# Bucketed attention and a rational feed-forward layer: sums, hash bits and a scaling put at other places in a hand-written order of work

## The chip, the cores and the metric

One core of one Trainium2 chip. The metric is the device time of one execution in microseconds (us). The kernel before took 917.11 us in the median of 3 runs (916.74 to 922.86).

## The reference

```python
# q, k, v: (4, 8, 768, 64); proj: (64, 6)
q_bucket = sum over 6 bits of 2**i * (q @ proj > 0)        # k_bucket likewise
mask = q_bucket[..., :, None] == k_bucket[..., None, :]
scores = where(mask, q @ k.T / 8, -1e9)
attn = exp(scores - max(scores)); attn /= sum(attn) + 1e-9
x = (attn @ v) laid out as (3072, 512)
# feed-forward: w_in (512, 2048), w_out (2048, 512), a (4), b (2)
h = x @ w_in
P = a0 + a1*h + a2*h*h + a3*h*h*h
Q = 1 + |b0|*|h| + |b1|*h*h
out = (P / (Q + 1e-6)) @ w_out
```

## The kernel before, in words

The 32 heads are worked on as 16 pairs, p = 0 to 15. A pair has 12 steps. A step (`scores`, lines 357 to 382) multiplies 128 keys with 384 queries for both heads, two matmuls a head (tile pss), and ScalarE takes the exponential of each head's 128x384 into one of nine buffers E. GpSimd adds the exponentials of six steps up into acc, one acc for each half of the queries (three acc buffers). `values` (384 to 391) multiplies a step's exponentials with v on a 64-column half of the TensorE array for each head (psv). In a middle pair (`group=6` in MID) the values of six steps are done in one go: steps 0 to 5 behind step 5, which are called the first values here, and steps 6 to 11 behind step 11, the second values. `values_out` (393 to 398) is ScalarE's scaling of the result into xo: a copy of one column (col) and an activation of 128x384. `values_store` sends xo to DRAM. `sums` (403 to 412) adds acc over its 128 rows with 32-column matmuls (psu, 8 matmul records) and copies the result to sr on ScalarE; `sums_store` sends it out in two DMAs of 3 KB; `recips` (421 to 432) reads it back for every fourth pair.

While pair p is worked on, later pairs are prepared. `load` (120 to 124) brings q and k, transposed, into qkf (two buffers). `high` (217 to 221) rounds them on ScalarE, `low` (227 to 230) takes the rest on VectorE, and `high_move`, `second_low`, `second_high` move halves between partitions by DMA. `bits` (244 to 257) multiplies q and k of two pairs with the projection (psb, 32 columns, 16 matmul records, in every other pair) and compares on VectorE; `penalties` and `maskrows` turn the bits into extra rows of q and k. `maxstep` (271 to 281) finds the row maxima: two matmuls (psm) and a VectorE reduction (m) for each of 12 steps. `shift_turn` transposes them (pst), `shift_rows` (294 to 300) puts them into a row of q by DMA.

The feed-forward weights are float64 and are converted in the same stretch (`weights`, 437 to 481, a generator of up to eight pieces: load, ScalarE pieces, VectorE pieces on the PSUM tile psx, a rounding with a PSUM copy psz, a subtraction, for w_out a store). After the attention comes the feed-forward layer: `Gemm1` (psh), the rational terms, `gemm2` (pso).

PSUM: the tag "s" has three banks, which pss, psu, psx, psz and the transposes share in turn; psm and psb share two double banks; psv has one bank. So the second head's scores of a step wait until the first head's exponential of the step before is done, three banks back.

The order of everything in the attention is written by hand. `at(p, s, f)` (487 to 488) puts a call at position 12 p + s, where s may be a fraction and may lie beyond the pair; all calls are sorted by position (608 to 610), and each engine and the DMA queue keep that order. The positions stand in the tables MID, FIRST (pairs 0 and 1 and what prepares pairs 0 to 2) and LAST (pairs 14 and 15). At the positions that matter here:

```python
at(p, s, scores, p, s)                                   # step s of pair p
at(p, s + MID["values"][s // n], values, p, i)           # 5.66 and 11.05
at(p, s + MID["values_out"][s // n], values_out, p, s // NT)   # 5.69 and 11.06
at(p, MID["sums"], sums, p)                              # 14.65: pair p+1, behind its third step
at(p - 2, MID["bits"], bits, p)                          # 2.81 of pair p-2
at(p - 2, MID["high"][1], high, p, 1)                    # k's rounding, 1.19 of pair p-2
at(p - 2, MID["low"][t + t * p % 2], low, p, t, ...)     # 1.06 and 3.3 or 3.35
```

Of the kernel before, what the change touches and what calls it, by code (L numbers as in the profile page):

```python
# [13 lines left out]
ALU = mybir.AluOpType  # L14
# [11 lines left out]
NPAIR = B * NHP  # L26
# [13 lines left out]
BANKED = (2, 29)  # L40

MID = dict(
    group=6, values=[0.66, 0.05], values_out=[0.69, 0.06],
    maxima=[6.54, 7.17, 8.32, 9.1, 10.1, 11.02, 12.25, 13.03, 14.15, 15.17, 16.01, 17.43], sums=14.65, sums_store=17.37,
    high=[-0.975, 1.19], low=[1.06, 3.3, 3.35], bits=2.81, penalties=4.02, high_move=1.9, maskrows=4.03, second_low=-2.2,
    second_high=2.69, load_v=10.99, shift_turn=5.67, shift_rows=8.82, load=4.04, recips=[20.0, 35.02, 35.3],
    weights=[[1.44, 5.1, 5.5, 5.65, 5.66, 11.02, 11.023], [8.05, 11.021, 11.022, 11.024, 11.0245, 17.63, 17.665, 19.32, 21.22]],
    weights_last=[0.5, 0.8, 1.0, 1.2],
)

FIRST = dict(
    maxima1=[-0.072, -0.05, 5.52, 5.97, 6.42, 6.87, 7.32, 7.77, 8.22, 8.67, 9.12, 9.57], maxima2=9.5, rate2=0.82, high=[3.25, 3.53],
    low=[6.0, 7.3], bits=7.4, penalties=7.45, high_move=4.53, maskrows=8.2, second_low=-24.19, second_high=4.35, load_v=4.78, group=2,
    values=[-1.07, 2.65, 2.32, 2.35, 0.35, 0.61], values_out=3.02, high1=[-3.0, -3.2], low1=[-2.8, -2.95],
    high_move1=-2.7, load2=-2.6, load3=3.8, load4=9.0, penalties1=-24.26, maskrows1=-24.2,
    weights=[[-27.25, 6.64, 6.7, 7.35, 12.19, 17.55, 18.33], [8.03, 9.04, 9.24, 9.25, 14.81, 15.27, 15.99, 17.91, 46.81]],
    warm0=9, warm1=1, warm=3, warms=[3, 3, 3, 0, 1, 0], maxima00=[-4.3, -2.3, -4.2, -0.9, -1.2, -0.8], shift00=[-1.0, -0.2],
    shift0=[-0.08, -0.075], ahead=3, scores=[[-0.85, -0.4, -0.1], [0.1, 0.3, 0.4]], pen01=[-2.9, -0.35],
    second_high0=[-3.42, -3.4, -3.3, -3.25], load_v0=-3.3, bits1=-0.3, comp1=[-0.28, -0.27],
    maxima0=[-24.05, -23.8, -23.5, -0.9, -0.7, -0.1], turn1=[8.46, 13.26], rows1=[9.59, 14.35], turn2=8.61, third=6.9,  # L60
    third_weights=[1.44, 5.1, 5.5, 5.65, 5.66, 11.02, 11.023], steps={3: -1.0, 4: -0.8, 5: -0.6, 6: 5.4, 7: 6.5},
)

LAST = dict(
    group=6, values=[0.28, 0.44], values_out=0.46, vout14=[3.5, 3.03],
    hi14=17.05, weights15=[5.1, 5.11],
    tokens=[[-15.0, -11.5, -8.6, -4.9], [-7.43, -4.5, -2.83, -1.09], [1.1, 4.2, 5.45, 6.3]], terms=1.0, ffn=[13.61, 16.09, 16.14],
    sums=16.96, wide=8, share=6, third=0, sums14=14.69, weights14=1.44, sumst14=22.46,
# [32 lines left out]
def move(nc, out, in_, queue=None):  # L101

    (queue or nc.sync).dma_start(out.bitcast(F32), in_.bitcast(F32))
# [3 lines left out]
def bucket_attention_then_rational_ffn(ctx, tc, qT, kT, v, proj, w_in, w_out, coef, consts, out):  # L107
# [56 lines left out]
    def operands_to_terms():  # L164
# [3 lines left out]

    tail.tile([P, 32], F32, tag="below", name="below")
    last = attention(tc, nc, raw, ps_b, tail, tokens, early, operands_to_terms, ffn, load, QF, KF, v, w_in, w_out, wo_d, ident, cst,  # L170
                     ones, prj, wi_hi, wi_lo, x_d, s_d, r_d, coefficients)
    ffn.rest(ctx, last)
# [3 lines left out]
def attention(ctx, tc, nc, raw, ps_b, tail, tokens, early, operands_to_terms, ffn, load, QF, KF, v, w_in, w_out, wo_d, ident, cst, ones, prj,  # L176
# [257 lines left out]
    def bank(name):  # L434
        return ps_b.tile([P, 512], F32, tag="s", bufs=3, name=name)

    def weights(i):

        if i % 2 == 0:
            f, cc = divmod(i // 2, 4)
            sl = slice(f * 512, f * 512 + 512)
            src, hi, lo = w_in[cc * P : cc * P + P, sl], wi_hi[:, cc, sl], wi_lo[:, cc, sl]
        else:
            src, hi, lo = w_out[i // 2 * P : i // 2 * P + P, :], None, None
        r = sm.tile([P, 2 * 512], F32, tag="wr", name=f"wr{i}", bufs=2)
        t = sm.tile([P, 512], F32, tag="ws", name=f"ws{i}", bufs=2)
        if src.dtype == F32:
            nc.sync.dma_start(t, src)  # L450
            yield
        else:
            nc.sync.dma_start(r.bitcast(I32), src.bitcast(I32))
            yield
            hw, lw = r[:, 1:1024:2], r[:, 0:1024:2]
            nc.scalar.activation(t, hw, AF.Copy, scale=2.0 ** -112)
            yield
            nc.scalar.activation(lw.bitcast(I32), lw.bitcast(U32), AF.Copy, scale=2.0 ** -29)
            x, y = hw.bitcast(I32), t.bitcast(I32)
            if BANKED[0] <= i < BANKED[1]:  # L460
                x = y = bank(f"psx{i}").bitcast(I32)
            nc.vector.tensor_scalar(out=x, in0=hw.bitcast(I32), scalar1=-(1 << 31), scalar2=None, op0=ALU.bitwise_and)
            yield
            nc.vector.scalar_tensor_tensor(out=y, in0=t.bitcast(I32), scalar=3, in1=x, op0=ALU.logical_shift_left,
                                           op1=ALU.bitwise_or)
            yield
            nc.vector.tensor_tensor(out=t.bitcast(I32), in0=y, in1=lw.bitcast(I32), op=ALU.add)
            yield
        if hi is None:
            hi, lo = r[:, 0:512].bitcast(F32R), r[:, 512:1024].bitcast(F32R)  # L470
        nc.scalar.copy(hi, t)
        z = hi.bitcast(F32)
        if BANKED[0] <= i < BANKED[1]:
            z = bank(f"psz{i}")
            nc.scalar.copy(z, hi.bitcast(F32))
        yield
        nc.vector.tensor_tensor(out=lo, in0=t, in1=z, op=ALU.subtract)
        yield
        if i % 2 == 1:
            move(nc, wo_d[i // 2], r.rearrange("p (t c) -> p t c", t=2))  # L480
            yield
# [5 lines left out]
    def at(p, s, f, *args):  # L487
        plan.setdefault(12 * p + s, []).append((f, args))

    def spread(p, steps, gen):  # L490
        for s in steps:
            at(p, s, lambda g: next(g, None), gen)

    for p in range(NPAIR):
        mid = 0 < p < NPAIR - 1
        n = MID["group"] if mid else (FIRST if p == 0 else LAST)["group"]
        for s in range(12):
            if p > 0 or s >= FIRST["ahead"]:
                at(p, FIRST["steps"].get(s, s) if p == 0 else s, scores, p, s)

            if p > 1:
                at(p - 2, FIRST["maxima2"] + FIRST["rate2"] * s if p == 2 else FIRST["third"] if p == 3 and s == 0 else MID["maxima"][s], maxstep, p, s)
            if s % n == n - 1:
                for i in range(s - n + 1, s + 1):
                    at(p, s + (MID["values"][s // n] if mid else (FIRST if p == 0 else LAST)["values"][s // n]), values, p, i)
            if s % NT == NT - 1:
                at(p, s + (LAST["vout14"][s // NT] if p == NPAIR - 2 else MID["values_out"][s // n] if mid else (FIRST if p == 0 else LAST)["values_out"]), values_out, p, s // NT)
        for hf in range(2):
            at(p, 6 * hf + 9, values_store, p, hf)
        if p < NPAIR - 1:  # L510
            at(p, MID["sums"] if p < NPAIR - 2 else LAST["sums14"], sums, p)
            at(p, MID["sums_store"] if p < NPAIR - 2 else LAST["sumst14"], sums_store, p)
        if p > 1:
            for t in range(2):
                at(p - 2, (MID if p > 2 else FIRST)["high"][t], high, p, t)
                at(p - 2, MID["low"][t + t * p % 2] if p > 2 else FIRST["low"][t], low, p, t, nc.vector if p > 2 else nc.gpsimd)
            if p % 2 == 0:
                at(p - 2, (MID if p > 2 else FIRST)["bits"], bits, p)
                at(p - 2, (MID if p > 2 else FIRST)["penalties"], penalties, p)
            at(p - 2, (MID if p > 2 else FIRST)["high_move"], high_move, p)  # L520
            at(p - 2, (MID if p > 2 else FIRST)["maskrows"], maskrows, p)
        if p > 0:
            at(p - 1, (MID if p > 1 else FIRST)["second_low"], second_low, p)
            at(p - 1, (MID if p > 1 else FIRST)["second_high"], second_high, p)
            at(p - 1, (MID if p > 1 else FIRST)["load_v"], load_v, p)
        if p > 1:
            at(p - 1, MID["shift_turn"] if p > 2 else FIRST["turn2"], shift_turn, p)
            at(p - 1, MID["shift_rows"], shift_rows, p)
        if p > 3:
            at(p - 4, MID["load"] if p > 4 else FIRST["load4"], load, p)  # L530
        if p % NHP == NHP - 1 and p + 1 < NPAIR:
            spread(p, MID["recips"], recips(p // NHP))
# [325 lines left out]
```

## Time and profile before

| | |
|---|---|
| median of 3 runs | 917.11 us (916.74 to 922.86) |
| profiled execution, its own time | 916.53 us |
| span of its instructions | 914.7 us |
| granted TensorE clock | 1.000 over the span |
| busy: TensorE, VectorE, ScalarE, GpSimd | 907.4, 818.0, 669.4, 438.7 us |

The span is from the first to the last instruction of the program; 1.8 us of the time lie around it. Durations of matmuls are modelled, and they overlap, so the distance from one start to the next tells what a matmul costs, not the duration of a row. A row of a timeline merges neighbouring instructions of the same kind. All times are us from the start of the span.

### The profile page before, as it was taken

The numbers are of one execution on the slowest core, as the hardware profiler recorded it, in microseconds if no ns is written. First come the engines' busy times: TensorE is split into PE (matmuls) and PEld (weight loads), VectorE is DVE, ScalarE is ACT, GpSimd is POOL, SyncE is SP. The second block draws the span as 40 slices with busy tenths as digits, with TensorE's granted clock in tenths as the row PEclk, the third lists the DMA queues.
The fourth block names the chain that finished last, engine by engine and source line by source line (L and its number), as shares of the span: only waits on it lengthen the run. The fifth ranks groups of instructions, "written<-read, shape, count | busy, mean of one in ns | idle before, by whom it ended". The sixth has DMA issues, their size and how long they took to land.

```text
span 914.7 us, 13736 instructions
## 1 busy us (share of the span) xinstructions
PE 907.4 (99%) x4543; PEld 694.8 (76%) x4543; DVE 818.0 (89%) x1043; ACT 669.4 (73%) x1254; POOL 438.7 (48%) x408
## 2 busy tenths in 40 slices
PE   9999999999999999999999999999999999999998
PEld 5567777676767676678888888888888888888886
DVE  7888888888888887989999999999999989998997
ACT  7467878887878787886677766776677677677664
POOL 7688888888888887012322232222322222222221
PEclk9999999999999999999999999999999999999999
DMA  7787878787878778456204000400040012001001
GB/s 215 202 217 226 235 213 248 218 244 212 242 224 241 195 215 242 137 202 198 95 1 138 1 1 1 138 1 1 0 138 1 1 56 83 1 1 47 1 0 47
DMA packets 51243, 111.57 MB, mean 122 GB/s; under 512 B 9346, under 2 KB 20214, under 8 KB 51172
## 3 DMA queue, kind: packets, MB, share of 16 engines
q1 hardware_dynamic: 50740, 110.47, 40.9%
q8 instruction: 36, 0.59, 0.3%
q14 instruction: 35, 0.29, 0.1%
q10 hardware_dynamic: 432, 0.23, 0.1%
HBM read 56.82 MB, written 21.17 MB: 85 GB/s over the span
## 4 chain that ended last, share of the span: by engine, by line
PE 97%; DVE 1%; DMA 1%; issue 0%; SPq 0%; ACT 0%; DVEq 0%
PE psh L96 29%; PE pso L96 29%; PE pss L96 15%; PE psv L96 14%; PE psm L96 7%; PE psu L96 1%; PE psb L96 1%; DVE m L96 1%; DMA qkf<-kT 0%; DMA k<-lo 0%; SPq L96 0%; PE pst_None L96 0%; PE pst L96 0%; PE psw L96 0%; DVE ws L96 0%
## 5 line engine op out<-in xcount | busy, mean ns | idle before, releaser
L96 POOL TENSOR_TENSOR gl<-c,gh 128x512 fp32r<-128x512 f32 x95 | 136.9, 1441 | 408.2 <-ACT gh L96 399.0
L96 PE MATMUL pso<-wo,gh 128*128 128x512 f32 x768 | 235.9, 389 | 0.0
L96 POOL TENSOR_TENSOR acc<-acc,E 128x384 f32<-128x384 f32 x232 | 219.6, 982 | 5.9 <-ACT E L96 5.8
L96 DVE TENSOR_REDUCE m<-psm 128x1 f32<-128x768 f32 x192 | 181.1, 954 | 46.1 <-PE psm L96 37.7
L96 ACT ACTIVATE E<-pss 128x384 f32<-128x384 f32 x384 | 167.5, 492 | 43.0 <-PE pss L96 28.4
L96 PE MATMUL pss<-q,k 128*128 128x384 f32 (+2 forms) x768 | 172.9, 348 | 0.1
L96 PEld LDWEIGHTS pso<-wo,gh 128*128 128x128 f32 x768 | 144.2, 188 | 29.9
L96 ACT ACTIVATE h<-psh 128x512 f32<-128x512 f32 x96 | 57.4, 598 | 133.7 <-PE psh L96 133.7
L96 PEld LDWEIGHTS pss<-q,k 128*128 128x128 f32 (+2 forms) x768 | 133.9, 189 | 24.4 <-issue 6.8
L96 PE MATMUL psh<-xh,wi_hi 128*128 128x512 f32 x384 | 149.6, 390 | 0.0
L96 PE MATMUL psh<-xh,wi_lo 128*128 128x512 f32 x384 | 149.4, 389 | 0.0
L96 PE MATMUL psh<-xl,wi_hi 128*128 128x512 f32 x384 | 149.4, 389 | 0.0
L96 PE MATMUL pso<-wo,gl 128*128 128x512 f32 x384 | 148.9, 389 | 0.0
L96 DVE SCALAR_TENSOR_TENSOR c<-c,ab,r 128x512 f32<-128x512 f32 x96 | 140.8, 1467 | 0.0
L96 PE MATMUL psv<-E,v 128*64 128x385 f32 x768 | 131.9, 492 | 0.0
L96 PE MATMUL psm<-k,q 76*128 76x384 f32 (+1 forms) x384 | 100.7, 344 | 2.0 <-DVE m L96 0.6
L96 PEld LDWEIGHTS psv<-E,v 128*64 128x64 f32 x768 | 52.0, 137 | 65.1 <-issue 63.3
L96 POOL TENSOR_TENSOR acc<-E,E 128x384 f32<-128x384 f32 x58 | 68.8, 1205 | 48.7 <-ACT E L96 48.7
L96 DVE SCALAR_TENSOR_TENSOR w<-h,absb,w 128x512 f32<-128x512 f32 x96 | 73.9, 770 | 16.2 <-ACT w L96 15.8
L96 PEld LDWEIGHTS psh<-xh,wi_hi 128*128 128x128 f32 x384 | 72.0, 187 | 16.1 <-ACT r L96 0.6
L96 PEld LDWEIGHTS psh<-xh,wi_lo 128*128 128x128 f32 x384 | 72.1, 188 | 15.0
L96 PEld LDWEIGHTS pso<-wo,gl 128*128 128x128 f32 x384 | 72.0, 188 | 15.0
(87 smaller groups left out, 1184.4 us busy)
## 6 DMA issues: line engine op xcount, KB each, us to landing
q<-q SPq DMA_DIRECT2D x45, 192.0 KB
k<-k SPq DMA_DIRECT2D x45, 192.0 KB
wr<-w_in SPq DMA_DIRECT2D x16, 512.0 KB
wr<-w_out SPq DMA_DIRECT2D x16, 512.0 KB
wo_d<-wr SPq DMA_DIRECT2D x16, 512.0 KB
wo<-wo_d SPq DMA_DIRECT2D x16, 512.0 KB
qkf<-qT SPq DMA_DIRECT2D x16, 384.0 KB
qkf<-kT SPq DMA_DIRECT2D x16, 384.0 KB
```

What stands on the lines that cost most here:

```text
L96: return self.tc.keep_in_program_order(issue(*args, **kwargs))
```

## The change

The positions of several calls are moved. `sums` of pair p goes from behind the third step of pair p+1 to directly ahead of that pair's first values (14.65 to 17.62), its store from 17.37 to 18.9, and the reading back from 20.0 to 21.5. `bits` goes from 2.81 of a pair to -0.945, directly behind the second values of the pair before it. The scaling of the second values goes from directly behind them (0.06) to behind the third step of the next pair (3.25), its store from 15 to 16.6. Three pieces of the even weights' conversion go from 5.5, 5.65 and 5.66 to 5.657, 5.658 and 5.659, behind the sums. In the first pairs: the pieces of weight 0 and its subtraction, the latter from VectorE to GpSimd; one DMA step of pair 1 (`rows1`, 9.59 to 8.6); the first `low` of pair 3 (1.06 to 1.9).

```diff
--- before.py
+++ after.py
@@ -40,11 +40,11 @@
 BANKED = (2, 29)
 
 MID = dict(
-    group=6, values=[0.66, 0.05], values_out=[0.69, 0.06],
-    maxima=[6.54, 7.17, 8.32, 9.1, 10.1, 11.02, 12.25, 13.03, 14.15, 15.17, 16.01, 17.43], sums=14.65, sums_store=17.37,
-    high=[-0.975, 1.19], low=[1.06, 3.3, 3.35], bits=2.81, penalties=4.02, high_move=1.9, maskrows=4.03, second_low=-2.2,
-    second_high=2.69, load_v=10.99, shift_turn=5.67, shift_rows=8.82, load=4.04, recips=[20.0, 35.02, 35.3],
-    weights=[[1.44, 5.1, 5.5, 5.65, 5.66, 11.02, 11.023], [8.05, 11.021, 11.022, 11.024, 11.0245, 17.63, 17.665, 19.32, 21.22]],
+    group=6, values=[0.66, 0.05], values_out=[0.69, 3.25],
+    maxima=[6.54, 7.17, 8.32, 9.1, 10.1, 11.02, 12.25, 13.03, 14.15, 15.17, 16.01, 17.43], sums=17.62, sums_store=18.9,
+    high=[-0.975, 1.19], low=[1.06, 3.3, 3.35], bits=-0.945, penalties=4.02, high_move=1.9, maskrows=4.03, second_low=-2.2,
+    second_high=2.69, load_v=10.99, shift_turn=5.67, shift_rows=8.82, load=4.04, recips=[21.5, 35.02, 35.3],
+    weights=[[1.44, 5.1, 5.657, 5.658, 5.659, 11.02, 11.023], [8.05, 11.021, 11.022, 11.024, 11.0245, 17.63, 17.665, 19.32, 21.22]],
     weights_last=[0.5, 0.8, 1.0, 1.2],
 )
 
@@ -53,13 +53,15 @@
     low=[6.0, 7.3], bits=7.4, penalties=7.45, high_move=4.53, maskrows=8.2, second_low=-24.19, second_high=4.35, load_v=4.78, group=2,
     values=[-1.07, 2.65, 2.32, 2.35, 0.35, 0.61], values_out=3.02, high1=[-3.0, -3.2], low1=[-2.8, -2.95],
     high_move1=-2.7, load2=-2.6, load3=3.8, load4=9.0, penalties1=-24.26, maskrows1=-24.2,
-    weights=[[-27.25, 6.64, 6.7, 7.35, 12.19, 17.55, 18.33], [8.03, 9.04, 9.24, 9.25, 14.81, 15.27, 15.99, 17.91, 46.81]],
+    weights=[[-27.25, 5.45, 5.98, 5.99, 11.9, 17.55, 18.3], [8.03, 9.04, 9.24, 9.25, 14.81, 15.27, 15.99, 17.91, 46.81]],
     warm0=9, warm1=1, warm=3, warms=[3, 3, 3, 0, 1, 0], maxima00=[-4.3, -2.3, -4.2, -0.9, -1.2, -0.8], shift00=[-1.0, -0.2],
     shift0=[-0.08, -0.075], ahead=3, scores=[[-0.85, -0.4, -0.1], [0.1, 0.3, 0.4]], pen01=[-2.9, -0.35],
     second_high0=[-3.42, -3.4, -3.3, -3.25], load_v0=-3.3, bits1=-0.3, comp1=[-0.28, -0.27],
-    maxima0=[-24.05, -23.8, -23.5, -0.9, -0.7, -0.1], turn1=[8.46, 13.26], rows1=[9.59, 14.35], turn2=8.61, third=6.9,
-    third_weights=[1.44, 5.1, 5.5, 5.65, 5.66, 11.02, 11.023], steps={3: -1.0, 4: -0.8, 5: -0.6, 6: 5.4, 7: 6.5},
+    maxima0=[-24.05, -23.8, -23.5, -0.9, -0.7, -0.1], turn1=[8.46, 13.26], rows1=[8.6, 14.35], turn2=8.61, third=6.9,
+    third_weights=[1.44, 5.1, 5.657, 5.658, 5.659, 11.02, 11.023], steps={3: -1.0, 4: -0.8, 5: -0.6, 6: 5.4, 7: 6.5},
 )
+
+FIRST3 = dict(low=[1.9, 3.3, 3.35])
 
 LAST = dict(
     group=6, values=[0.28, 0.44], values_out=0.46, vout14=[3.5, 3.03],
@@ -474,7 +476,7 @@
             z = bank(f"psz{i}")
             nc.scalar.copy(z, hi.bitcast(F32))
         yield
-        nc.vector.tensor_tensor(out=lo, in0=t, in1=z, op=ALU.subtract)
+        (nc.vector if i else nc.gpsimd).tensor_tensor(out=lo, in0=t, in1=z, op=ALU.subtract)
         yield
         if i % 2 == 1:
             move(nc, wo_d[i // 2], r.rearrange("p (t c) -> p t c", t=2))
@@ -506,14 +508,14 @@
             if s % NT == NT - 1:
                 at(p, s + (LAST["vout14"][s // NT] if p == NPAIR - 2 else MID["values_out"][s // n] if mid else (FIRST if p == 0 else LAST)["values_out"]), values_out, p, s // NT)
         for hf in range(2):
-            at(p, 6 * hf + 9, values_store, p, hf)
+            at(p, 16.6 if hf and p < NPAIR - 2 else 6 * hf + 9, values_store, p, hf)
         if p < NPAIR - 1:
             at(p, MID["sums"] if p < NPAIR - 2 else LAST["sums14"], sums, p)
             at(p, MID["sums_store"] if p < NPAIR - 2 else LAST["sumst14"], sums_store, p)
         if p > 1:
             for t in range(2):
                 at(p - 2, (MID if p > 2 else FIRST)["high"][t], high, p, t)
-                at(p - 2, MID["low"][t + t * p % 2] if p > 2 else FIRST["low"][t], low, p, t, nc.vector if p > 2 else nc.gpsimd)
+                at(p - 2, (MID if p > 3 else FIRST3)["low"][t + t * p % 2] if p > 2 else FIRST["low"][t], low, p, t, nc.vector if p > 2 else nc.gpsimd)
             if p % 2 == 0:
                 at(p - 2, (MID if p > 2 else FIRST)["bits"], bits, p)
                 at(p - 2, (MID if p > 2 else FIRST)["penalties"], penalties, p)
```

## Rows read from the trace of the kernel before

**Rows 1.** The page: busy time, share of the span and instructions of each engine, and the shares of each engine in the chain that ended last.

```profile
PE 907.4 (99%) x4543; PEld 694.8 (76%) x4543; DVE 818.0 (89%) x1043; ACT 669.4 (73%) x1254; POOL 438.7 (48%) x408
...
PE 97%; DVE 1%; DMA 1%; issue 0%; SPq 0%; ACT 0%; DVEq 0%
```

**Rows 2.** Timeline of TensorE's matmuls (PE), one pair of heads in which no hash bits are computed. Columns: start in us, duration in us, engine, line, operation, out<-in, tile and shape, count of instructions merged into the row; in brackets the idle time ahead of it and what ended it.

```profile
190.29 0.88 PE L96 MATMUL pss<-q,k 77*128 77x384 f32 x4
191.01 0.51 PE L96 MATMUL psm<-k,q 76*128 76x384 f32 x2
191.45 0.85 PE L96 MATMUL psu<-acc,ones 128*32 128x384 f32 x8
192.23 0.97 PE L96 MATMUL pss<-q,k 77*128 77x384 f32 x4
193.04 0.51 PE L96 MATMUL psm<-k,q 76*128 76x384 f32 x2
193.39 0.88 PE L96 MATMUL pss<-q,k 77*128 77x384 f32 x4
...
195.62 4.10 PE L96 MATMUL psv<-E,v 128*64 128x385 f32 x24
199.65 0.27 PE L96 MATMUL pst_None<-cst,m 128*12 128x128 f32 x1
...
200.89 0.52 PE L96 MATMUL psm<-k,q 76*128 76x384 f32 x2
```

**Rows 3.** The same view of TensorE, the next pair, in which hash bits (psb) are computed.

```profile
214.05 0.85 PE L96 MATMUL psu<-acc,ones 128*32 128x384 f32 x8
214.72 1.47 PE L96 MATMUL psb<-qkf,prj 128*32 128x384 f32 x16
216.12 0.97 PE L96 MATMUL pss<-q,k 77*128 77x384 f32 x4
...
223.51 0.28 PE L96 MATMUL pst_None<-cst,m 128*12 128x128 f32 x1
...
224.46 0.52 PE L96 MATMUL psm<-k,q 76*128 76x384 f32 x2
```

**Rows 4.** Timeline of ScalarE (ACT), the pair of rows 2; same columns.

```profile
188.21 0.16 ACT L96 COPY col<-psv 128x1 f32<-128x1 f32 x1 [0.77 <-PE psv L96]
188.40 0.58 ACT L96 ACTIVATE xo<-psv,col 128x384 f32<-128x384 f32 x1
188.88 1.84 ACT L96 ACTIVATE E<-pss 128x384 f32<-128x384 f32 x4
190.60 0.83 ACT L96 CAST k<-qkf 128x768 fp32r<-128x768 f32 x1
191.32 0.88 ACT L96 ACTIVATE E<-pss 128x384 f32<-128x384 f32 x2
```

**Rows 5.** Timeline of ScalarE in pair 14, where a conversion of token data (xh<-y) stands among the exponentials.

```profile
354.77 0.83 ACT L96 CAST xh<-y 128x768 fp32r<-128x768 f32 x1
355.50 1.76 ACT L96 ACTIVATE E<-pss 128x384 f32<-128x384 f32 x4
```

**Rows 6.** Timeline of TensorE in pair 14, the same moments as rows 5.

```profile
354.46 0.86 PE L96 MATMUL pss<-q,k 77*128 77x384 f32 x4
355.16 0.52 PE L96 MATMUL psm<-k,q 76*128 76x384 f32 x2
355.51 1.16 PE L96 MATMUL pss<-q,k 77*128 77x384 f32 x4
356.51 0.52 PE L96 MATMUL psm<-k,q 76*128 76x384 f32 x2
```

**Rows 7.** Timeline of VectorE (DVE), the pair of rows 2.

```profile
193.59 0.96 DVE L96 TENSOR_REDUCE m<-psm 128x1 f32<-128x768 f32 x1 [0.41 <-PE psm L96]
...
199.69 0.68 DVE L96 TENSOR_TENSOR wr<-ws,psz 128x512 fp32r<-128x512 f32 x1
```

**Rows 8.** Timeline of TensorE in the first two pairs.

```profile
46.29 0.62 PE L96 MATMUL psm<-k,q 76*128 76x384 f32 x2
46.93 0.97 PE L96 MATMUL pss<-q,k 77*128 77x384 f32 x4
...
54.54 0.61 PE L96 MATMUL psm<-k,q 76*128 76x384 f32 x2 [0.61 <-DVE m L96]
...
61.94 0.87 PE L96 MATMUL pss<-q,k 77*128 77x384 f32 x4
62.95 0.62 PE L96 MATMUL psm<-k,q 76*128 76x384 f32 x2
```

**Rows 9.** Timeline of VectorE in pair 1.

```profile
61.35 0.68 DVE L96 TENSOR_TENSOR wi_lo<-ws,wi_hi 128x512 fp32r<-128x512 f32 x1
```

**Rows 10.** Timeline of the sync engine's DMA queue (SPq) in pair 0 and in the pair of rows 2; the duration is that of the issue, not of the transfer.

```profile
41.61 2.13 SPq L96 DMA_DIRECT2D qkf<-kT  x1
43.85 1.42 SPq L96 DMA_DIRECT2D q<-mt  x2
...
199.72 0.42 SPq L96 DMA_DIRECT2D qkf<-kT  x1
```

**Rows 11.** The view of one tile, the transposed q and k of a pair (qkf): operation and count, shortest, median and longest duration in ns, first and last start in us.

```profile
L96 ACT CAST q<-qkf x17: 814/823/843, 3.8 to 325.7; 128x768 fp32r<-128x768 f32 x16, 64x768 fp32r<-64x768 f32 x1
...
L96 SPq DMA_DIRECT2D qkf<-qT x16: 386/486/563, 0.7 to 291.4; - x16
```

## Prediction, written before the changed kernel was run

> **What bounds the kernel now.** I read the page first: TensorE is busy for 907.4 of 914.7 us and holds 97% of the chain that ended last [rows 1]. So the time can fall only where TensorE's starts come further apart than its work needs, and it rises with every wait put in its way. The timelines of TensorE show such places, since durations in them overlap and the distance of starts counts. With no wait, from the scores of a step (pss) to the maxima (psm) is 0.72 us, and from there to the next scores 0.35 [rows 2]: 1.07 us a step. A visit to narrow matmuls costs more than its work. In a pair without bits, psm at 191.01 is followed by the sums (psu) at 191.45, scores at 192.23, psm at 193.04; without the sums that psm would have come at 191.01 + 0.35 + 0.72 = 192.08. The visit costs 0.96 us. The sums alone take 214.72 - 214.05 = 0.67, where more narrow work follows [rows 3]. The other 0.29 is entering and leaving. The timelines of ScalarE, VectorE and the DMA queue came next, to see who ends TensorE's waits once the order is different.
>
> **A. Fewer visits: -4.1 us.** Before, a pair has three narrow visits: first values, second values, and the sums, with the bits behind them in every other pair. Afterwards the sums stand ahead of the first values and the bits behind the second, so two are left. The work stays: 0.67 for the sums, and 216.12 - 214.72 = 1.40 for the bits with their exit, which takes the place of the values' exit. Sums of pairs 0 to 13 move: 14 x 0.29 = 4.1 us. The trace has no sums beside values. I take the change from one to the other as free, as it is from sums to bits (0.67, two groups of four). If it costs 0.1 us, a third of a visit's overhead, 2.7 is left; if entering the values gets 0.05 cheaper, 4.8.
> The trace counts against a page of the Trainium skill here. "TensorE: Matmul & The Clock Gate", section "The cost: per-tile semaphore tail", says that column tiles which each report their end to a semaphore report one after another, by a fitted formula; for the four reports of the sums it gives 149 ns, as an estimate. By it the visit would keep that tail and A would be 2.1 us smaller; by the row of sums and bits it is not seen.
>
> **B. ScalarE without its pauses: +5.6 us.** Where the sums stood, TensorE left the scores alone for 0.87 us (1.4 more with bits), and ScalarE caught up. Now steps 0 to 5 run straight on, and ScalarE has two other pieces among their exponentials: k's rounding (0.83), which was there, and the scaling of the second values, now behind the third step.
> First piece: the rounding at 190.60 puts the third step's exponentials to 191.32 [rows 4]; two take 0.88, so the first ends near 191.8. Without the sums, the fourth step's scores start at 191.36 and the second head's at 191.71, and these need that bank. They wait about 0.15 with the semaphore, and some 0.1 is lost on restarting. Pair 14 shows just this: a conversion of 0.83 at 354.77 puts exponentials to 355.50 [rows 5], and the scores at 355.51 are followed by psm after 1.00 us where the step before took 0.70 [rows 6]. I take that price, 0.29.
> Second piece: column and scaling push the next exponentials by 188.88 - 188.21 = 0.67. The fourth step's first would start near 192.76 and end at 193.25; the fifth step's second head wants the bank at 191.36 + 1.07 + 0.35 + 0.29 = 193.07. That is 0.23 late with the semaphore, and 0.12 for restarting: 0.35. No row has two such pieces so close together, and TensorE may have slipped behind by other waits. Between 0 and 0.35 I take the middle, 0.18.
> The rounding and the scaling both stand in pairs 2 to 13: 12 x 0.47 = 5.6 us; the bounds are 0 and 12 x 0.64 = 7.7. At the old place the scaling costs TensorE nothing: the exponentials behind it start at 188.88, some 0.1 late, and the banks cover that. What it now holds up on ScalarE is queued behind it in order, the exponentials and then the weights' pieces.
>
> **C. VectorE's lateness behind the first values: -3.3 us.** Behind the values come the transpose (pst), scores and psm. With nothing in the way this is 0.72 and 0.10 for leaving, 0.82 us. It is 1.24 in the pair without bits (199.65 to 200.89) [rows 2] and 0.95 in the one with them (223.51 to 224.46) [rows 3]. What is late is the weights' conversion, which holds banks of the tag "s"; its subtraction starts at 199.69, after the transpose [rows 7]. Six pairs of each kind lose 6 x 0.42 + 6 x 0.13 = 3.3 us. Afterwards TensorE comes there later by 0.67 - 0.96 + 0.47 = 0.18, while VectorE no longer sits idle for the sums (0.41 ahead of 193.59) [rows 7] and has no comparison among its reductions. I take all of it as regained. The other bound is nothing: without B's waits TensorE is 0.29 early instead, and the lateness stays. The new order of the pieces (5.657 and on) only follows from the sums' place: they take the bank first.
>
> **D. First pairs: -0.7 us.** In pair 0, psm at 46.29 is followed by scores at 46.93, 0.64 later [rows 8], where 0.35 and 0.10 for leaving the values would do; with the restart I count 0.28. The row of maxima that these scores need is sent at 43.85, behind a load whose issue takes 2.13 us [rows 10]; from 8.6 it passes that load. In pair 1, psm at 62.95 comes 1.01 behind its scores, 0.29 over 0.72 and 0.1 for restarting: VectorE subtracts wi_lo at 61.35 [rows 9], which goes to GpSimd, idle then. That is 0.4. The wait of 0.61 at 54.54 I leave: the pieces of weight 0 and low's move free VectorE of some 0.7, and the sums' leaving takes 0.96 of its time to catch up. Bounds for all of D: -1.8 and +0.5.
>
> **Moves at no cost.** The bits need both pairs' q and k. The last load is issued by 200.14 [rows 10], and the bits would come some three steps and a switch ahead of where the sums stood (214.05 [rows 3]), near 210.7; the very first cast starts 3.1 us behind its load's issue (0.7 to 3.8) [rows 11]. Of these 10 us about 7 are cover; if they were gone, the excess would stand before every other pair's scores. The values' store (one DMA) passes the six DMAs of rows and load on the queue, the sums' store (two) passes none, the reading back (one) passes a weight's load, the row of maxima and a store; what reads them comes many steps later. The sums' copy on ScalarE falls under 4 us of values. acc is needed again six steps after the sums' new place begins, at the seventh step; three buffers cover it.
>
> **Sum.** -4.1 + 5.6 - 3.3 - 0.7 = -2.5 us on the profiled execution's own time of 916.53 (span 914.7), so 914.0. The median of the runs lies 0.58 above that execution: **914.6 us**. A measurement of this kernel can tell about 1%, 9.2 us, from no change; the forecast lies within that.
>
> **Rivals.** 1, ScalarE keeps up (chance 0.2): the banks absorb both pieces and B is 0, with C regained all the same: 914.6 - 5.6 = **909.0 us**; 912.3 if VectorE's lateness stays. For it: ScalarE is busy for 669 of 915 us. Against: pair 14.
> 2, ScalarE becomes the bound of steps 0 to 5 (0.2), the slower side: both pieces cost their full 0.64 in 12 pairs, and the weights' pieces behind them reach VectorE as late as before, so C is nothing: -4.1 + 7.7 - 0.7 = +2.9, which with the 0.58 is **920.0 us**. It decides from the point where a pair loses more to waits for E than the 0.29 of the visit and the 0.28 that C is worth. For it: all its terms have rows. Against: TensorE, once late, gives both engines time.
> 3, the narrow groups don't join (0.05): every change from sums to values costs 0.15, so A is 14 x 0.15 = 2.1 smaller: 916.7.
> 4, the change doesn't do what it says (0.03): bits wait for a load after all and hold the scores, in six pairs by 0.5 or more: 914.6 + 3.0 = 917.6 and up.
> My own case has 0.5; the remaining 0.02 is for what I don't see.
>
> **Range and chances.** A from 2.7 to 4.8, B from 0 to 7.7, C from 0 to 3.3 and D from -1.8 to +0.5 span 907 to 922; they won't all end at one side. 909 to 921 holds my case, most of rivals 1 and 2, and 3 and 4. Faster by over 1% (under 907.9) needs rival 1 with every gain: 0.06. Slower by over 1% (over 926.3) is beyond every case worked out: 0.03. Within 1%: 0.91.
>
> **What would show it.** Right: in TensorE's timeline psu directly ahead of psv, psb directly behind it, each without a gap of over 0.4; between two first values two visits, not three. B right: steps 3 and 4 of a pair (psm to psm) stretched to 1.2 to 1.4 us, the third-step exponentials still near 3.3 us behind the pair's first scores, and waits for E where there were none. B wrong: steps 0 to 5 all at 1.07. C right: 0.82 from pst to psm. D right: 0.45 at the first scores of pair 1. The forecast is wrong if TensorE's share of the chain falls, or a pair's length grows by over 0.3 us.

## The result and the profile after

The changed kernel takes **925.44 us** in the median of 6 runs (924.46 to 926.77), the kernel before 917.22 beside it: a ratio of 1.0086 (95% interval 1.0068 to 1.0103), 0.9% slower. Forecast were 914.6 us and a range from 909 to 921. The profiled execution took 925.1 us over a span of 923.3, at a granted clock of 1.00.

The page of the changed kernel, busy times and the chain by engine; they answer to [rows 1]:

```profile
PE 912.7 (99%) x4543; PEld 693.3 (75%) x4543; DVE 820.4 (89%) x1042; ACT 667.6 (72%) x1254; POOL 438.8 (48%) x409
...
PE 95%; DVE 2%; ACT 1%; DMA 1%; issue 1%; SPq 0%; ACTq 0%; DVEq 0%
```

ScalarE does no more work than before, yet it now stands in the chain. The waits of TensorE's weight loads (PEld) for the exponentials say how: us in total, times, longest. First the kernel before, then the changed one:

```profile
PEld pss L96 <- ACT E L96: 6.2, 13, 0.6
```

```profile
PEld pss L98 <- ACT E L98: 15.5, 39, 2.1
```

Three times as many waits, 9.3 us more. Where they stand shows in TensorE's timeline: the first scores of pair 1 and a wait of 1.75 us in the same pair, then steps 1 to 7 of pair 6, an ordinary one, and the second values of pair 7 with the bits behind them; this answers to [rows 2, 3]. Steps are counted from 0 to 11 here, so the third step is step 2; the expectations below count from 1.

```profile
47.88 0.62 PE L98 MATMUL psm<-k,q 76*128 76x384 f32 x2
48.33 0.88 PE L98 MATMUL pss<-q,k 77*128 77x384 f32 x4
...
52.87 0.52 PE L98 MATMUL pss<-q,k 77*128 77x384 f32 x2
55.15 0.62 PE L98 MATMUL pss<-q,k 77*128 77x384 f32 x2 [1.75 <-ACT E L98]
...
172.13 0.52 PE L98 MATMUL psm<-k,q 76*128 76x384 f32 x2
...
173.19 0.52 PE L98 MATMUL psm<-k,q 76*128 76x384 f32 x2
173.55 1.15 PE L98 MATMUL pss<-q,k 77*128 77x384 f32 x4
174.53 0.52 PE L98 MATMUL psm<-k,q 76*128 76x384 f32 x2
174.89 1.23 PE L98 MATMUL pss<-q,k 77*128 77x384 f32 x4
175.96 0.51 PE L98 MATMUL psm<-k,q 76*128 76x384 f32 x2
...
177.03 0.51 PE L98 MATMUL psm<-k,q 76*128 76x384 f32 x2
177.47 0.85 PE L98 MATMUL psu<-acc,ones 128*32 128x384 f32 x8
178.25 4.10 PE L98 MATMUL psv<-E,v 128*64 128x385 f32 x24
182.28 0.28 PE L98 MATMUL pst_None<-cst,m 128*12 128x128 f32 x1
...
183.11 0.52 PE L98 MATMUL psm<-k,q 76*128 76x384 f32 x2
183.63 0.97 PE L98 MATMUL pss<-q,k 77*128 77x384 f32 x4
...
212.63 4.10 PE L98 MATMUL psv<-E,v 128*64 128x385 f32 x24
216.66 1.50 PE L98 MATMUL psb<-qkf,prj 128*32 128x384 f32 x16
218.09 0.97 PE L98 MATMUL pss<-q,k 77*128 77x384 f32 x4
```

Read it by starts. The maxima of steps 1 and 2 are 1.06 apart; then come 1.34 and 1.43, and 1.07 again. ScalarE's timeline, which answers to [rows 4], names both pieces (its first line belongs to pair 1 and to experiment 8, the last three to the first values of pair 6):

```profile
53.85 0.20 ACT L98 ACTIVATE absb<-ab 128x1 f32<-128x1 f32 x1 [1.46 <-DMA ab<-coef]
...
172.80 0.83 ACT L98 CAST k<-qkf 128x768 fp32r<-128x768 f32 x1
173.52 0.88 ACT L98 ACTIVATE E<-pss 128x384 f32<-128x384 f32 x2
174.28 0.18 ACT L98 COPY col<-psv 128x1 f32<-128x1 f32 x1
174.49 0.58 ACT L98 ACTIVATE xo<-psv,col 128x384 f32<-128x384 f32 x1
174.97 1.69 ACT L98 ACTIVATE E<-pss 128x384 f32<-128x384 f32 x4
...
182.42 0.16 ACT L98 COPY col<-psv 128x1 f32<-128x1 f32 x1 [1.50 <-PE psv L98]
182.61 0.58 ACT L98 ACTIVATE xo<-psv,col 128x384 f32<-128x384 f32 x1
183.10 0.86 ACT L98 ACTIVATE E<-pss 128x384 f32<-128x384 f32 x2
```

The rounding (172.80) puts off the exponentials of the third step, the scaling (174.28) those of the fourth, before ScalarE has caught up.

**The bill by steps.** From the timelines of TensorE I took the distance between the starts of the maxima of neighbouring steps, as a mean over the time in which pairs 3 to 12 are worked on (five have bits in them before, and five after). The other steps are within 0.05 of one another. "2 to 3" holds the sums and bits of the kernel before, "5 to 6" the first values, and "11 to 0" the second values. The last rows are experiments that come below.

| kernel | 2 to 3 | 3 to 4 | 4 to 5 | 5 to 6 | 6 to 7 | 11 to 0 |
|---|---|---|---|---|---|---|
| before | 2.68 | 1.06 | 1.06 | 5.55 | 1.07 | 5.28 |
| after | 1.35 | 1.45 | 1.07 | 6.12 | 1.22 | 6.00 |
| experiment 1, e1_scaling_back | 1.34 | 1.06 | 1.06 | 6.08 | 1.25 | 6.00 |
| experiment 2, e3_scaling_alone | 2.68 | 1.07 | 1.06 | 5.52 | 1.07 | 5.29 |
| experiment 3, e2_sums_alone | 2.04 | 1.06 | 1.06 | 6.08 | 1.19 | 5.29 |
| experiment 5, e6_rounding_moved | 1.06 | 1.34 | 1.16 | 6.16 | 1.20 | 6.00 |
| experiment 6, e7_no_first | 1.34 | 1.07 | 1.06 | 6.09 | 1.25 | 6.00 |

By the starts of the scores these ten pairs take 230.83 us before and 236.18 after, 5.35 more. The rest of the 8.6 us between the two spans: 1.07 ahead of the first scores of all (12.55 and 13.62; this differs between executions, 13.54 in experiment 3 and 12.54 in experiment 6), 0.33 in pair 0, 1.61 in pairs 1 and 2, 0.21 behind pair 12.

### The profile page after: what moved, and what is told of

It reads as the page before. It is cut to its first block, busy times and chain, and to the rows that moved or that the text cites. A ratio compares the mean times of both kernels' runs of the same rounds, so it can differ in the third digit from the quotient of the medians.

```text
span 923.3 us, 13754 instructions
## 1 busy us (share of the span) xinstructions
PE 912.7 (99%) x4543; PEld 693.3 (75%) x4543; DVE 820.4 (89%) x1042; ACT 667.6 (72%) x1254; POOL 438.8 (48%) x409
## 4 chain that ended last, share of the span: by engine, by line
PE 95%; DVE 2%; ACT 1%; DMA 1%; issue 1%; SPq 0%; ACTq 0%; DVEq 0%
PE psh L98 28%; PE pso L98 28%; PE pss L98 14%; PE psv L98 13%; PE psm L98 6%; PE psu L98 1%; PE psb L98 1%; ACT E L98 1%; DVE m L98 1%; PE psw L98 1%; DMA ab<-coef 1%; DMA q<-q 0%; SPq L98 0%; DVE lo L98 0%; PE pst_None L98 0%
## 5 line engine op out<-in xcount | busy, mean ns | idle before, releaser
L98 PE MATMUL pss<-q,k 128*128 128x384 f32 (+2 forms) x768 | 177.1, 349 | 3.6 <-ACT E L98 2.1
L98 DVE SCALAR_TENSOR_TENSOR c<-c,ab,r 128x512 f32<-128x512 f32 x96 | 138.7, 1445 | 0.0
L98 POOL TENSOR_TENSOR acc<-E,E 128x384 f32<-128x384 f32 x58 | 66.7, 1168 | 54.5 <-ACT E L98 54.5
L98 PEld LDWEIGHTS psh<-xl,wi_hi 128*128 128x128 f32 x384 | 72.0, 188 | 14.9
```

The source lines that it names most:

```text
L98: return self.tc.keep_in_program_order(issue(*args, **kwargs))
```

## The experiments

Theory: ScalarE pays for the two pieces in full, A and C give less than forecast, and the first pairs cost. Rivals: the first pairs alone, the queue, VectorE. All were timed beside the kernel before; times are medians.

**1. The scaling put back.**

```diff
 (after)
-    values_out=[0.69, 3.25]
+    values_out=[0.69, 0.06]
```

> The changed kernel with only the scaling of the second values back at 0.06, directly behind them. Theory (ScalarE's two pieces among the exponentials hold TensorE's scores: 0.29 us a pair between steps 3 and 4 by k's rounding, 0.44 between steps 4 and 5 by the scaling): the step from 4 to 5 falls from 1.50 to about 1.07 in pairs 2 to 13, the step from 3 to 4 keeps its 1.35; 12 x 0.44 = 5.3 us faster than the changed kernel, about 920. Rival (the loss comes from the new places of sums and bits, whoever's exponentials are late): no change, 925.

Measured: 920.44 us, ratio 1.0040 (1.0026 to 1.0054); 5.0 less than the changed kernel. Three to four falls from 1.45 to 1.06, all of its excess. The scaling at its new place is the largest single loss. In TensorE's timeline the rounding's wait stays (195.16 to 196.48, 1.32) and the scaling's is gone (1.08):

```profile
195.16 0.51 PE L98 MATMUL psm<-k,q 76*128 76x384 f32 x2
195.51 1.13 PE L98 MATMUL pss<-q,k 77*128 77x384 f32 x4
196.48 0.52 PE L98 MATMUL psm<-k,q 76*128 76x384 f32 x2
196.83 0.88 PE L98 MATMUL pss<-q,k 77*128 77x384 f32 x4
197.56 0.51 PE L98 MATMUL psm<-k,q 76*128 76x384 f32 x2
```

**2. Only the scaling moved.**

```diff
 (before)
-    values_out=[0.69, 0.06]
+    values_out=[0.69, 3.25]
-            at(p, 6 * hf + 9, values_store, p, hf)
+            at(p, 16.6 if hf and p < NPAIR - 2 else 6 * hf + 9, values_store, p, hf)
```

> The kernel before with only the scaling of the second values moved to 3.25 and its store to 16.6; sums and bits stay between the third and fourth step. Theory: the sums' visit still gives ScalarE its pause, so the scaling falls into it and costs at most 0.15 a pair: 916 to 919. Rival (the scaling at 3.25 holds TensorE by itself, whatever stands beside it): 0.44 a pair, 921 to 922.5.

Measured: 917.72 us, ratio 1.0014 (1.0003 to 1.0024), and 3 to 4 at 1.07. The same scaling at the same position costs 0.39 a pair without the sums' pause ahead of it (0.37 in nine of the ten pairs, 0.64 in pair 7) and 0.01 with it. The loss is one of the two moves together.

**3. Only the sums moved** (and the even weights' three pieces behind them).

```diff
 (before)
-    ... sums=14.65, sums_store=17.37, ... recips=[20.0, ...
+    ... sums=17.62, sums_store=18.9, ... recips=[21.5, ...
-    weights=[[1.44, 5.1, 5.5, 5.65, 5.66, ...
+    weights=[[1.44, 5.1, 5.657, 5.658, 5.659, ...
```

> The kernel before with the sums alone moved (17.62, store 18.9, read back 21.5, and the even weights' three pieces behind them); bits, scaling and first pairs as before. Theory: a pair without bits loses 0.29 us to k's rounding, since nothing separates steps 2 and 3 any more, and gains some 0.18 from the visit saved; a pair with bits keeps its separation by the bits and neither gains nor loses over 0.1. Total within 1.5 us of the kernel before: 916 to 918.5. Rival (the sums ahead of the first values cost by themselves): 4 us or more slower, 921 and up.

Measured: 917.54 us, ratio 1.0012 (1.0003 to 1.0021). The bits keep a visit of their own here, so the gain of a visit is there in half of the pairs. In these five the rounding's wait (2 to 3 is 1.32 to 1.34 there, up to 0.28 over a plain step) and one behind the first values (6 to 7 is 1.32 to 1.34) take back what the visit and C give.

**4. Only the first pairs' moves** (pieces of weight 0, the third pair's residue, the row at 8.6, weight 0's subtraction on GpSimd).

> The kernel before with only the work of the first pairs moved (weight 0's pieces, its subtraction on GpSimd, pair 1's row of maxima sent earlier, pair 3's first low later). The changed kernel stands 3.1 us later at pair 2's first scores. Theory A: that loss comes from the sums' leaving, which exposes ScalarE's wait for the coefficients' DMA in pair 1; then this kernel is 0 to 1 us faster than before, 916 to 917. Theory B: the moved first work causes it: 2 to 3 us slower than before, 919 to 920.5.

Measured: 918.57 us, 1.65 more than before, ratio 1.0022 (1.0013 to 1.0031), between both theories. The moves cost by themselves; 9 to 12 part them.

**5. The rounding moved as well.**

```diff
 (after, scaling at 0.06)
-    high=[-0.975, 1.19]
+    high=[-0.975, -0.97]
```

> The changed kernel with the scaling back at 0.06 and k's rounding beside q's, behind the second values' start (-0.97 instead of 1.19), so that ScalarE has only exponentials in steps 0 to 5 until the penalties. Theory: both waits go, steps 3 to 4 and 4 to 5 take 1.07 each; 12 x 0.73 = 8.8 us faster than the changed kernel, 916.6, a little less if VectorE's lateness behind the first values comes back (up to 0.28 a pair, 919 to 920). Rival (the places of sums and bits cost): 925.

Measured: 922.73 us, ratio 1.0066 (1.0054 to 1.0079): a miss for both sides. The rounding's wait did go (2 to 3 is 1.06), so it is what stretched that step. But 3 to 4 became 1.34: with ScalarE out of the way VectorE is late. The waits of the maxima's weight loads here, 12.0 us in 24 waits against 8.3 in 14 of experiment 1, and, as a second fence, one of them in pair 5 with VectorE's residue of q ahead of it:

```profile
PEld psm L98 <- DVE m L98: 12.0, 24, 1.4
```

```profile
149.59 1.76 DVE L98 TENSOR_TENSOR lo<-qkf,q 128x768 fp32r<-128x768 f32 x1
152.27 0.61 PE L98 MATMUL psm<-k,q 76*128 76x384 f32 x2 [0.77 <-DVE m L98]
```

The mean hides two kinds of pairs. In pairs 3 and 5 that residue takes 1.73 and 1.76 us and 3 to 4 takes 1.95 and 2.00; in the other eight it takes 0.95, and 3 to 4 takes 1.16 to 1.19. The granted clock is a part of the miss too: it was 0.996 to 0.998 in the mean of each of these executions, and at its lower level for some 3.4 us of pair 1 in the profiled one.

**6. Sums and bits alone** (after, with the scaling and the first pairs as before).

> The changed kernel with the scaling back at 0.06 and the work of the first pairs as before: only the new places of sums (with the weights' pieces) and bits are left. Theory: k's rounding still stands among the exponentials, 0.29 a pair in 12 pairs, against the visits saved, which are worth less than I forecast since going from 32-column to 64-column matmuls costs some 0.1: within 1.5 us of the kernel before, 917 to 918.5; the 920.4 of the run with only the scaling back falls by what the first pairs' moves cost alone (1.7) or more, since TensorE's clock need not fall in pair 1. Rival (bits behind the second values cost by themselves): 920 or more.

Measured: 918.44 us, ratio 1.0026 (1.0012 to 1.0040). Merging the visits, without any of the rest, gains nothing: by the table a pair saves 1.34 between steps 2 and 3, with the rounding's wait already in it, and pays 0.54 and 0.72 at the two places where sums and bits now stand, and 0.18 behind the first values. Taken off one after the other, the moves make up the 8.2 us to within 0.1: 5.0 by the scaling (experiment 1), 2.0 by the first pairs' work (920.44 to 918.44) and 1.3 by sums and bits.

**7. Both engines made lighter in steps 2 to 5.**

```diff
 (experiment 6)
-    high=[-0.975, 1.19], low=[1.06, 3.3, 3.35], ... load=4.04
+    high=[-0.975, -0.97], low=[1.06, 6.3, 6.35], ... load=6.4
```

> As the run before (sums and bits moved, scaling at 0.06, first pairs as before), and in addition k's rounding beside q's (-0.97), the low part of k on VectorE behind the first values (6.3 instead of 3.3), and the load that takes over its buffer behind that (6.4 instead of 4.04). Theory (in steps 0 to 5, once nothing separates them, ScalarE's and VectorE's extra pieces hold TensorE, and moving k's rounding alone only uncovered VectorE): steps 0 to 5 take 1.07 each with no wait on E or on maxima; 3 to 4 us faster than the run before, 913 to 915, faster than both kernels. Rival (steps are bounded by something else, or the second half now waits): no gain, 917 or more.

Measured: 946.69 us, ratio 1.0312 (1.0276 to 1.0347): missed by over 30 us, on the other side. k's residue, now at 6.3, reads the buffer that the load at 6.4 (qkf<-qT) overwrites, and the DMA queue keeps its order. The queue in pair 2, in experiment 6 and then here (durations are those of the issues), with VectorE's residue of k here as a third fence:

```profile
84.54 0.45 SPq L98 DMA_DIRECT2D qkf<-qT  x1
...
87.65 0.38 SPq L98 DMA_DIRECT2D wr<-w_out  x1
```

```profile
84.84 0.52 SPq L98 DMA_DIRECT2D x_d<-xo  x1
88.09 0.33 SPq L98 DMA_DIRECT2D qkf<-qT  x1
...
91.17 0.38 SPq L98 DMA_DIRECT2D wr<-w_out  x1
```

```profile
87.08 0.95 DVE L98 TENSOR_TENSOR lo<-qkf,k 128x768 fp32r<-128x768 f32 x1
```

The residue ends at 88.03 and the load goes out at 88.09; until then the queue stands still, and the weight's load behind it goes out 3.5 us later than in experiment 6 (the pair began 0.8 later). Its pieces come late on both engines and hold banks of "s": ScalarE and VectorE wait 22.5 and 25.3 us in all for that load. The granted clock fell as well (0.979 to 0.993 in the mean of single executions; in the profiled one some 13.7 us from 301 us on lie at its lower level, an estimated 7 of the 26.6 us by which its span is longer than that of experiment 6). What the steps themselves would have gained can't be read from this run.

**8. The coefficients earlier.** In pair 1 the exponential behind 53.85 waits for a small load.

```diff
 (after)
-    spread(1, (0, 2), coefficients())
+    spread(1, (-5.5, 2), coefficients())
```

> The changed kernel with the coefficients' DMA 5.5 steps earlier on the queue (pair 1, -5.5 instead of 0), so that ScalarE does not wait 1.46 us for it in pair 1. Theory: the wait of 1.75 us on E in pair 1 goes, VectorE's lateness there gives back a part: 0.7 to 2 us faster than the changed kernel, 923.3 to 924.7. Rival (VectorE is the bound of that stretch in any case): within 0.5 of 925.3.

Measured: 924.99 us, ratio 1.0086 (1.0073 to 1.0099). The wait for the load is gone, and the maxima at 55.61 wait 0.85 for VectorE instead. Nothing gained: the longest wait in the profile had another one behind it.

**9 to 12. The first pairs' moves apart.**

```diff
 (9: before, pieces and the third pair's residue)
-    weights=[[-27.25, 6.64, 6.7, 7.35, 12.19, 17.55, 18.33], ...
+    weights=[[-27.25, 5.45, 5.98, 5.99, 11.9, 17.55, 18.3], ...
+FIRST3 = dict(low=[1.9, 3.3, 3.35])
 ...
 (10: before, the row)
-    ... rows1=[9.59, 14.35], ...
+    ... rows1=[8.6, 14.35], ...
 (11: before, weight 0's subtraction; 12: 10 and 11)
-        nc.vector.tensor_tensor(out=lo, in0=t, in1=z, op=ALU.subtract)
+        (nc.vector if i else nc.gpsimd).tensor_tensor(out=lo, in0=t, in1=z, op=ALU.subtract)
```

> The kernel before, with two of the four moves of the first pairs: the pieces of weight 0 at steps 5.45, 5.98, 5.99, 11.9 and 18.3, and the third pair's first rounding residue at 1.9. All first-pair moves together gave 918.57 against 916.92, 1.65 more. Theory P: the pieces do it; the 1.39 us piece of weight 0 (ws) goes on VectorE ahead of three reductions at 31.12 instead of behind them, so the maxima at 33.43 come 0.85 and 0.41 late where the kernel before waits 0.64 once, and in the second pair the residues meet GpSimd and take 1.7 us each. Then this kernel is 0.8 to 1.7 us over the kernel before, and the other three are within 0.5 of it. Rival L: weight 0's residue on GpSimd does it, and this kernel is within 0.5.

> The kernel before, with the first row of maxima sent at 8.6 instead of 9.59 and nothing else. Both theories: the wait at the first scores of the second pair (46.93, 0.18 over the mean spacing) goes; 0 to 0.4 us less than the kernel before if nothing behind it is late, and nothing if VectorE is what ends the next waits.

> The kernel before, with the subtraction for weight 0's residue (wi_lo at 61.35) on GpSimd instead of VectorE and nothing else. Forecast of the record: 0.4 less. Theory P: within 0.5 of the kernel before. Rival L: GpSimd's subtraction takes longer and slows VectorE beside it, the maxima at 62.7 are late by 0.9 instead of 0.3, and the kernel is 0.6 to 1.5 us over the kernel before.

> The kernel before, with the row at 8.6 and weight 0's residue on GpSimd, the two moves for which the record counts a gain of 0.7 us. Theory P: 0 to 0.7 less than the kernel before, so perhaps the fastest of all. Rival L: 0.4 to 1.5 more.

Measured, beside 917.02 for the kernel before: pieces 918.41, ratio 1.0023 (1.0009 to 1.0037); row 918.88, 1.0019 (1.0006 to 1.0032); subtraction 916.30, 0.9996 (0.9987 to 1.0005); row and subtraction 920.72, 1.0026 (1.0010 to 1.0042). So the pieces cost, as theory P had it, and the subtraction does not. (Of the pieces' twelve executions nine kept a mean granted clock of 1.000 and lie at 917.2 to 919.3; the profiled one, 923.04, did not.) The row is a miss for both theories, and why shows in the single times: with the row moved they lie in two groups, six at 916.6 to 918.0 and six at 919.8 to 921.4; with the subtraction too, four at 915.8 to 916.5 and eight at 920.3 to 921.9. The mean granted clock of the single executions parts the same groups: 0.999 and 1.000 in both lower ones, 0.995 to 0.998 and 0.996 in the upper ones. The profiled execution of the row alone is of the upper group, that of row and subtraction of the lower. Its stretches of 2 us: TensorE busy (records), granted clock, share of the DMA engines, GB/s.

```profile
54.00:56.00 2.00, 1.70 (x8) 1.00 0.54 118
56.00:58.00 2.00, 0.92 (x5) 1.00 0.99 203
58.00:60.00 2.00, 2.00 (x9) 0.56 0.97 182
60.00:62.00 2.00, 2.00 (x10) 0.58 0.46 143
62.00:64.00 2.00, 2.00 (x14) 1.00 0.45 63
```

The maxima of 57.08 wait 1.31 us for VectorE, and right behind them the clock falls to its lower level, 1.2 GHz, for some 3.4 us: the first values take 5.72 instead of 4.10. With row and subtraction the wait at this place is 0.62 and the clock stays. Pair 1 takes 28.43 and 24.75 us in these two, so 1.6 of the 3.7 between them lie at the lower clock, the rest mostly in waits ahead of it. An idle TensorE alone doesn't decide it, since the changed kernel was profiled with more of it and kept the clock:

```profile
52.00:54.00 2.00, 1.39 (x8) 1.00 0.90 272
54.00:56.00 2.00, 0.85 (x5) 1.00 0.96 176
56.00:58.00 2.00, 2.00 (x17) 1.00 1.03 237
```

No experiment points to a version that beats the kernel before: the subtraction alone is within the measurement's error of it.

## Why the prediction was wrong

By steps, for one of the pairs 3 to 12, forecast and measured (from the table): A -0.29 and -0.11; B +0.47 and +0.70; C -0.28 and -0.07; with 0.02 in steps 0 to 2 the sum is +0.54, where -0.10 was forecast. Over the kernel A came out 2.3 us worse than forecast, B 3.1 and C 2.5, and D 2.4 by experiment 4: 10.3 of the 10.8 us by which the forecast was missed. The miss is not one term's: all four came out worse, and each has a step of its own that failed.

**A, half wrong.** The visits are two instead of three, as forecast. The step that failed is "I take the change from one to the other as free, as it is from sums to bits". From the sums to the values it is 177.47 to 178.25, 0.78 instead of the 0.67 of [rows 3]: this join of 32-column to 64-column groups costs 0.1, and the visit saves 0.19, the bound of 2.7 us that I had worked out and put aside. It costs again from the values to the bits, which I did not price: values to bits to scores is 216.66 - 212.63 = 4.03 and 218.09 - 216.66 = 1.43, where the bits behind the sums added 1.28 (by the table of starts, pairs with and without). Two like groups side by side were given up for two unlike ones. That it is the width that costs is read from these rows alone; no run varies it by itself. Over the kernel A is about 14 x -0.19 + 6 x 0.15 = -1.8 us instead of -4.1.

**B, right in mechanism, mis-sized.** Both waits stand where they were looked for, waits for E with steps of 1.34 and 1.43. The first was forecast at 0.29 and is 0.28 (1.34 less 1.06 in experiment 6). The second I cut from 0.35 to 0.18, since TensorE might have slipped behind by other waits. That cut is the step that failed: TensorE had not slipped behind, and the scaling costs 0.37 in nine of the ten pairs, just above the bound, and 0.64 in pair 7, where VectorE's residue is slow as well. By experiments 1 and 2 it is there only without the pause. The bound of 7.7 would have been nearer than the 5.6; over pairs 2 to 13 B is 8.7.

**C, right at its place, given back at the next.** From the transpose to the maxima it is 183.11 - 182.28 = 0.83, as forecast, in 10 of the 12 pairs 2 to 13. What failed is the step "I take all of it as regained". In six of the twelve pairs the next scores come 0.52 behind these maxima instead of 0.35: they wait for an exponential that stands behind the scaling of the first values (182.61, 183.10). VectorE's lateness had covered ScalarE's. In the table: 5 to 6 grows by 0.57 with sums that add 0.79, and 6 to 7 by 0.15. Of the 3.3 us 0.8 is left.

**D, wrong in sign.** The wait at the scores of pair 1 went (48.33 is 0.45 behind 47.88 in the changed kernel, the sign that I had named). But I priced no piece for what it is put ahead of, and that is the step that failed: by experiment 4 the moves of D cost 1.65 us together, where I counted a gain of 0.7. By experiment 9 the pieces alone cost 1.4 us (2.1 by the ratio). The subtraction agrees with its 0.4 within the error. The row, 0.28 by my count, costs 1.9 in the median, through those executions in which a longer wait for VectorE and a fall of the clock follow; neither was in my sum.

**The rivals.** Rival 2 had the side and the mechanism, and its deciding point held: a pair loses 0.85 to waits for E (B and the wait behind the first values) against the 0.57 that it named. Its 920.0 falls short by 5.4: by A's size (2.3), by D (2.4) and by B's size (1.0), less the 0.8 that C gave after all; 0.5 stays open. Rival 3, a price for the joint, was right too, at 0.11 instead of 0.15; I gave it a chance by itself, but it came together with rival 2. Rivals 1 and 4 are excluded: the banks did not cover the pieces, and no bits wait for a load in the rows.

By my own list the sign that I was wrong was a pair that grows by over 0.3 us; it grew by 0.54, and TensorE's share of the chain fell from 97 to 95%.

The clock is not what makes the changed kernel slower: both profiled executions kept 1.00 from end to end and lie 8.6 us apart (916.53 and 925.1); the three of the changed kernel at 0.998 in the mean lie at 925.8 to 926.8.

Open: why the clock falls in some executions and not in others; and how the pieces of weight 0 share their cost between pair 0 and the residues of pair 1.

## What to carry to other kernels

A short stop of the busiest engine can be the time in which the next one catches up; before it is removed, add up what that engine must do between the two places, and take the full price when the pieces stand a step apart. Merge visits so that groups of the same width lie side by side, and price each joint from the nearest row. On a queue that keeps its order, a later producer is a later everything behind it.

## What the runs showed of the hardware

- In these rows narrow matmul groups join freely only where they are alike: 0.67 from the 32-column sums to the 32-column bits [rows 3], 0.78 from the sums to the 64-column values.
- The granted clock fell to 1.2 GHz for some 3.4 us behind a wait for VectorE in pair 1, and not in the profiled execution of a kernel that differs by one subtraction; the single times of either lie in two groups 3.5 to 4.7 us apart.
- VectorE's rounding residue (lo, 128x768) takes 0.95 to 1.16 us in pairs 3 to 13 of the changed kernel but for pair 7, where it is 1.73 and 1.82 (at 196.62 and 200.00), with GpSimd adding beside it in either case. In pair 2 too it was 1.79 and 1.83, and these are the two pairs in which C was not regained (1.22 and 1.18 from the transpose to the maxima). What decides is how much is left of the GpSimd add that runs when the residue starts. First a slow residue (pair 7), then a quick one (pair 6), each with the adds beside it:

```profile
196.51 1.01 POOL L98 TENSOR_TENSOR acc<-E,E 128x384 f32<-128x384 f32 x1
196.62 1.73 DVE L98 TENSOR_TENSOR lo<-qkf,q 128x768 fp32r<-128x768 f32 x1
```

```profile
172.61 1.02 POOL L98 TENSOR_TENSOR acc<-E,E 128x384 f32<-128x384 f32 x1 [2.89 <-ACT E L98]
173.56 0.95 DVE L98 TENSOR_TENSOR lo<-qkf,q 128x768 fp32r<-128x768 f32 x1
173.59 1.80 POOL L98 TENSOR_TENSOR acc<-E,E 128x384 f32<-128x384 f32 x1
```

  At 196.62 the add has 0.90 us left, at 173.56 it has 0.07; the residues take 0.83 and 0.88 us more than that. In all 26 residues of the changed kernel this remainder is 0.81 to 0.90, so the residue waits for the add, and the add that starts behind it (173.59) waits in turn and takes 1.80 instead of 1.02.
